# Value steps and w_down: the narrow operand as a broadcast of 32 columns

## The chip, the cores and the metric

The kernel runs on one core of one Trainium2 chip. The metric is the device time of one execution in microseconds (us). The time before is the median of 8 runs. A profile is one execution, taken by the hardware profiler; its span goes from the first to the last instruction.

## The reference

Four layers follow each other on x of shape (4, 1, 512): attention, feed-forward, attention, feed-forward. Both attention layers use the same caches and weights, and so do both feed-forward layers. Cut to what matters:

```python
def _A_ref(x, k_cache, v_cache, wq, wo):      # 32 query heads, 8 kv heads, 4096 keys, head size 128
    q = (x @ wq).reshape(B, 1, 32, 128).transpose(0, 2, 1, 3)
    k = jnp.repeat(k_cache, 4, axis=1)
    v = jnp.repeat(v_cache, 4, axis=1)
    p = softmax(einsum("bhqd,bhkd->bhqk", q, k) * 128 ** -0.5)
    o = einsum("bhqk,bhkd->bhqd", p, v)
    return o.transpose(0, 2, 1, 3).reshape(B, 1, 4096) @ wo

def _B_ref(x, w_gate, w_up, w_down):          # 512 -> 1792 -> 512
    return (gelu(x @ w_gate) * (x @ w_up)) @ w_down

x = x + _A_ref(layernorm(x), ...)
x = x + _B_ref(layernorm(x), ...)
x = x + _A_ref(layernorm(x), ...)
x = x + _B_ref(layernorm(x), ...)
```

All tensors are bf16. The batch B is 4, so each of the four sequences has its own K and V caches of 8 MB each; a K or V tile of half a kv head is 512 KB.

## The kernel before, in words

**Rounds.** The order of all work is written out by hand. Round `attend(b2, b1)` runs the first attention layer of sequence b1 and, beside it, the second attention layer of sequence b2 = b1 - 1, while the K tiles of b1 replace those of b2. K is read once for each sequence and kept in `KT` (8 kv heads x 2 tiles), V is read twice, through a ring of `KV_BUFS` = 7 buffers (two tiles of sequence 0 are kept). Before each round, `dense(b, 1)` runs the end of the output projection, the feed-forward layer and the next q for one sequence; value steps of the attention layer still open (`fill`) are put between its pieces. At the end `attend_last` runs the second attention of the last sequence, and `dense(0, 4)` the last feed-forward layer for all four sequences.

**Queues.** Nearly all loads are issued by SyncE's queue, in program order: `Keys.load` (L365) for K, `load_v` (L461) for V, `load_wq` (L122) and `load_rest` (L127 to L133) for the weights. A K load waits until the scores have read the tile it replaces, a V load until a value step has given a buffer back.

**Attention.** VectorE turns each K tile in place (L372). `scores` (L383) multiplies with moving tiles of 512 columns, four 32-column groups of the array side by side. `soft` takes the maximum (L389 to L398) and the exponential (ScalarE, L402). `soft_turn` (L410) and `soft_swap` (L429, L432) bring the probabilities to the partitions that the values need, `soft_den` (L415) and `soft_recip` (L420) give the denominators.

**Value steps.** `Values.step` takes one V tile. It is the stationary operand: 16 matmuls (L481), each with a new 128 x 128 piece of V as weights and 4 moving columns, the probabilities of the 4 query heads of that kv head at one key position per partition. Two tiles, 32 matmuls, accumulate into four columns of `ot`. VectorE multiplies with the inverse denominators and writes bf16 (L489), mostly for two kv heads at once.

**Projections.** `out_proj` (L280) and `q_rows` (L225) use the activation as weights and stream 512 columns of wo or wq, four column groups side by side; `ffn_in` does so with 448 columns of w_gate and w_up (L314), or, for four sequences at once, with the weights stationary and 4 moving columns (L307). `turn_rows` (L215) turns the rows to columns. `y_select` (L268) and `out_proj_end` (L286) finish the projection in the tile `y`.

**w_down.** `down` (L347) runs 14 x 4 matmuls with pieces of w_down stationary and `nb` moving columns, 1 in the rounds and 4 in the last layer; `add_y` (L293, L297) adds the result to x.

## Time and profile before

| what | value |
|---|---|
| median of 8 runs | 316.94 us (314.24 to 319.25) |
| the profiled execution | 319.25 us |
| its span | 317.4 us |
| TensorE matmul busy | 212.3 us (67%) |
| VectorE busy | 171.3 us (54%) |
| ScalarE busy | 28.9 us (9%) |
| moved by DMA | 114.09 MB, mean 359 GB/s over the span |
| share of DMA time used by the load queue | 94.0% |
| mean granted TensorE clock | 0.703 |

Matmul rows are read in this way: each matmul takes longer than the spacing to the next one, since they are pipelined, so the time of a row of matmuls is the spacing times their number and the length of the last one. PE is TensorE's matmuls, PEld its weight loads, DVE VectorE, ACT ScalarE, SPq the queue of SyncE that issues the loads. In the slices of the page each digit is a fortieth of the span, 7.9 us. "PEclk" is the granted clock of TensorE. The chain of waits is followed back from the last instruction; the view of waits gives, for each pair, the total time waited in us, how often, and the longest wait.

### The profile page before, as it was taken

The page shows a single profiled execution, that of the slowest core. Times are in us where ns is not written, and L with a number is a line of the kernel's source. Part 1 is how long each engine was busy: PE and PEld are TensorE (multiplying, and loading weights), DVE is VectorE, ACT ScalarE, POOL GpSimd, SP SyncE. Part 2 cuts the span into 40 slices and gives each one's busy share as a digit, 9 for nine tenths or more (in the row PEclk, how much of TensorE's full clock was granted, in tenths as well). Part 3 has the DMA queues.
Part 4 walks back from the last instruction along what each step waited for, and adds up shares of the span by engine and source line. Part 5 has one row for each costly group of instructions (what it writes and reads, how often), then busy time and mean ns, then how long its engine had stood idle before and what let it go on. Part 6 is the DMA issues. An engine that isn't in the chain of part 4 may idle for free.

```text
span 317.4 us, 8714 instructions
## 1 busy us (share of the span) xinstructions
PE 212.3 (67%) x3844; PEld 121.7 (38%) x3844; DVE 171.3 (54%) x481; ACT 28.9 (9%) x70; POOL 0.7 (0%) x6
## 2 busy tenths in 40 slices
PE   1460585243677669889864389799762877998875
PEld 0010344121324135656330246464411455645654
DVE  5575751014338896355487944454799543545133
ACT  0002001000002021200100203000202040002100
POOL 0000000000000000000000000000000000000000
PEclk9999999999998555556875555555855555559555
DMA  7999999999949999999999999999999999999900
GB/s 261 374 412 399 407 410 403 351 379 383 391 124 363 405 409 405 359 387 409 357 411 408 409 390 334 378 379 370 359 410 409 408 393 348 398 389 381 392 15 3
DMA packets 35526, 114.09 MB, mean 359 GB/s; under 512 B 3224, under 2 KB 9120, under 8 KB 35488
## 3 DMA queue, kind: packets, MB, share of 16 engines
q1 hardware_dynamic: 35488, 113.53, 94.0%
q8 instruction: 30, 0.49, 0.6%
q14 instruction: 8, 0.07, 0.1%
HBM read 113.51 MB, written 0.00 MB: 358 GB/s over the span
## 4 chain that ended last, share of the span: by engine, by line
DMA 47%; PE 24%; DVE 15%; SPq 9%; issue 3%; ACT 1%; DVEq 0%; ACTq 0%
DMA kt<-in_A_k_cache_dram 23%; DMA v<-in_A_v_cache_dram 21%; PE sc L383 6%; PE ot L481 6%; DVE kt L372 5%; PE rows L314 3%; DMA wd_sb<-in_B_w_down_dram 3%; SPq L127 3%; SPq L133 3%; PE rows L280 3%; PE y L347 2%; PE rows L225 1%; PE x L429 1%; DVE rows L215 1%; DVE pp L410 1%
## 5 line engine op out<-in xcount | busy, mean ns | idle before, releaser
L372 DVE STREAM_TRANSPOSE kt<-kt 128x1024 f32<-128x1024 f32 x64 | 75.1, 1216 | 7.4 <-DMA kt<-in_A_k_cache_dram 7.3
L481 PEld LDWEIGHTS <-v 128*128 128x128 bf16 x1920 | 59.6, 104 | 50.6 <-DMA v<-in_A_v_cache_dram 25.7
L481 PE MATMUL ot<-pe,v 128*128 128x4 bf16 x1920 | 63.7, 166 | 19.7 <-DMA v<-in_A_v_cache_dram 18.8
L383 PE MATMUL sc<-kt,qb 128*32 128x512 bf16 x512 | 63.5, 550 | 17.1 <-DVE kt L372 13.1
L215 DVE STREAM_TRANSPOSE rows<-rows 128x512 f32<-128x512 f32 (+1 forms) x23 | 16.3, 707 | 39.2 <-PE rows L225 19.7
L383 PEld LDWEIGHTS <-qb 128*32 128x32 bf16 x512 | 17.3, 116 | 47.7 <-issue 30.7
L402 ACT ACTIVATE pp<-sc,nm 128x512 bf16<-128x512 f32 x16 | 11.0, 688 | 154.5 <-DVE junk L398 154.5
L489 DVE TENSOR_TENSOR OT_bf<-ot,rden 128x8 bf16<-128x8 f32 (+1 forms) x40 | 6.5, 162 | 34.2 <-PE ot L481 33.8
L429 PE MATMUL x<-pp,ident_bf 128*32 128x128 bf16 x256 | 9.1, 284 | 23.4 <-DVE pp L410 23.2
L280 PE MATMUL rows<-wo_sb,OT_bf 128*1 128x512 bf16 (+1 forms) x136 | 17.2, 611 | 7.4 <-DMA wo_sb<-in_A_wo_dram 6.4
L225 PE MATMUL rows<-wq_sb,xn_bf 128*1 128x512 bf16 (+1 forms) x160 | 18.5, 609 | 4.9 <-DMA wq_sb<-in_A_wq_dram 4.5
L429 PEld LDWEIGHTS <-ident_bf 128*32 128x32 bf16 x256 | 6.7, 122 | 29.5 <-issue 27.8
L389 DVE TENSOR_REDUCE m<-sc 128x1 f32<-128x512 f32 x16 | 10.8, 675 | 12.3 <-PE sc L383 12.3
L410 DVE STREAM_TRANSPOSE pp<-pp 128x512 bf16<-128x512 bf16 x16 | 11.2, 701 | 4.6 <-ACT pp L402 4.3
L432 ACT CAST pe<-x 128x512 bf16<-128x512 f32 x16 | 9.4, 585 | 21.5 <-PE x L429 21.5
L347 PE MATMUL y<-H_bf,wd_sb 128*128 128x1 bf16 (+1 forms) x280 | 8.4, 165 | 2.8 <-DVE H_bf L340 1.6
L246 PE MATMUL qe<-qm,t_bf 128*128 128x64 bf16 x16 | 3.4, 212 | 10.2 <-DVE qm L236 6.2
L249 DVE TENSOR_TENSOR qb<-qe,amask 128x256 bf16<-128x256 f32 x16 | 6.8, 424 | 5.4 <-PE qe L246 5.4
L347 PEld LDWEIGHTS <-wd_sb 128*128 128x128 bf16 x280 | 8.0, 103 | 4.1 <-DMA wd_sb<-in_B_w_down_dram 3.0
L225 PEld LDWEIGHTS <-xn_bf 128*1 128x1 bf16 (+1 forms) x160 | 4.3, 108 | 13.2 <-issue 12.1
L415 PE MATMUL den<-zx,mean_f 128*128 128x16 f32 x32 | 8.9, 357 | 0.0
L420 DVE RECIPROCAL rden<-den 128x16 f32<-128x16 f32 x16 | 4.0, 251 | 8.8 <-PE den L415 8.3
(78 smaller groups left out, 124.4 us busy)
## 6 DMA issues: line engine op xcount, KB each, us to landing
v<-in_A_v_cache_dram SPq DMA_DIRECT2D x118, 512.0 KB, 8.7
kt<-in_A_k_cache_dram SPq DMA_DIRECT2D x64, 512.0 KB, 11.0
wq_sb<-in_A_wq_dram SPq DMA_DIRECT2D x2, 2048.0 KB, 7.8
wo_sb<-in_A_wo_dram SPq DMA_DIRECT2D x4, 1024.0 KB, 12.0
kt<-in_A_v_cache_dram SPq DMA_DIRECT2D x8, 512.0 KB, 9.2
wg_sb<-in_B_w_gate_dram SPq DMA_DIRECT2D x1, 1792.0 KB, 13.5
wu_sb<-in_B_w_up_dram SPq DMA_DIRECT2D x1, 1792.0 KB
wd_sb<-in_B_w_down_dram SPq DMA_DIRECT2D x1, 896.0 KB, 16.1
```

The costliest lines, as they stand in the source:

```text
L127: dq.dma_start(out=wo_sb[:, i * n:(i + 1) * n], in_=wo_dram[:, i * n:(i + 1) * n])
L215: nc.vector.transpose(out=rows[:, :n], in_=rows[:, :n])
L225: nc.tensor.matmul(rows[j * QS:j * QS + nb, :], lhsT=xn_bf[:, k, bs], rhs=w, start=(k == 0), stop=(k == KD - 1))
L280: nc.tensor.matmul(rows[r0:r0 + lhsT.shape[-1], :], lhsT=lhsT, rhs=wo_sb[:, i, :], start=(start and n < QD), stop=(stop and n >= hp - QD))
L347: nc.tensor.matmul(y[:, k], lhsT=wd_sb[:, c, k * P:(k + 1) * P], rhs=H_bf[:, c, :], start=(c == 0 and k == 0), stop=(c == KF - 1), skip_gr ...
L372: nc.vector.transpose(out=words, in_=words)
L383: nc.tensor.matmul(sc[s * QS:(s + 1) * QS], lhsT=qb[:, w0:w0 + 2 * W], rhs=kt[:, :, be // 2, :, be % 2], start=(t == 0 and be == 0), stop= ...
L389: nc.vector.tensor_reduce(out=m[:], in_=sc.rearrange("p c j -> p (c j)"), axis=AX.X, op=ALU.max)
L402: nc.scalar.activation(out=pp[:], in_=sc[:], func=ACT.Exp, bias=nm[:, 0:1], scale=scale, accum_out=ls[:])
L410: nc.vector.transpose(out=flat, in_=flat)
L429: nc.tensor.matmul(x[a * QS:(a + 1) * QS, s], lhsT=ident_bf[:, s * QS:(s + 1) * QS], rhs=pT[:, a], start=True, stop=True, skip_group_check ...
L481: nc.tensor.matmul(self.ot[:, s % 2], lhsT=v[:, i, :], rhs=pe[:, s, c, :], start=(c == 0), stop=(c == C - 1), skip_group_check=True)
```

## The change

Both kinds of matmul with a narrow moving operand get 32 moving columns. In a value step the 4 columns are read eight times over by a broadcast dimension of stride 0, and in `down` the 1 or 4 columns 32 or 8 times. The PSUM tiles grow by the same factor, from 8 to 64 fp32 per partition for `ot`, from 4 or 16 to 128 for `y` of `down`, and hold as many equal copies of the result; one copy is read. The number of instructions, the stationary operands, the order and the loads are as before.

```diff
+    WIDE = 8
...
     def down(nb, H_bf):
-        y = ps_sm.tile([P, KD, nb], FP32, name="y", tag="sm")
+        n = WIDE * rep // nb
+        y = ps_sm.tile([P, KD, n, nb], FP32, name="y", tag="sm")
         for c in range(KF):
             for k in range(KD):
-                nc.tensor.matmul(y[:, k], lhsT=wd_sb[:, c, k * P:(k + 1) * P], rhs=H_bf[:, c, :],
+                nc.tensor.matmul(y[:, k], lhsT=wd_sb[:, c, k * P:(k + 1) * P],
+                                 rhs=H_bf[:, c, :].unsqueeze(1).broadcast_to([P, n, nb]),
                                  start=(c == 0 and k == 0), stop=(c == KF - 1), skip_group_check=True)
-        return y
+        return y[:, :, 0]
...
-                    self.ot = ps_ot.tile([P, 2, rep], FP32, name="ot", tag="ot")
+                    self.ot = ps_ot.tile([P, 2, WIDE, rep], FP32, name="ot", tag="ot")
...
-                    nc.tensor.matmul(self.ot[:, s % 2], lhsT=v[:, i, :], rhs=pe[:, s, c, :],
+                    rhs = pe[:, s, c, :].unsqueeze(1).broadcast_to([P, WIDE, rep])
+                    nc.tensor.matmul(self.ot[:, s % 2], lhsT=v[:, i, :], rhs=rhs,
                                      start=(c == 0), stop=(c == C - 1), skip_group_check=True)
...
-                        in0=self.ot[:, s0 % 2:s0 % 2 + m], in1=rden[:, s0:s0 + m], op=ALU.mult)
+                        in0=self.ot[:, s0 % 2:s0 % 2 + m, 0], in1=rden[:, s0:s0 + m], op=ALU.mult)
```

## The prediction

> **What bounds the kernel now.** I read the page first: its slices, its costliest groups, and the waits of the DMA queue.

> ```profile
> PEclk9999999999998555556875555555855555559555
> DMA  7999999999949999999999999999999999999900
> GB/s 261 374 412 399 407 410 403 351 379 383 391 124 363 405 409 405 359 387 409 357 411 408 409 390 334 378 379 370 359 410 409 408 393 348 398 389 381 392 15 3
> ...
> L481 PEld LDWEIGHTS <-v 128*128 128x128 bf16 x1920 | 59.6, 104 | 50.6 <-DMA v<-in_A_v_cache_dram 25.7
> L481 PE MATMUL ot<-pe,v 128*128 128x4 bf16 x1920 | 63.7, 166 | 19.7 <-DMA v<-in_A_v_cache_dram 18.8
> ```

> ```profile
> SPq L461 <- PE ot L481: 72.2, 60, 3.1
> ```

> Transfers bound it: 113.5 MB run at about 408 GB/s wherever nothing holds them, 278 us of a 317.4 us span. TensorE has two roles beside that. It frees the V buffers (the second fence: the queue waits for ot), so its pauses let the rate fall to 330 to 390 GB/s, and it carries the end, where the last 16 us move no data.

> The clock row needs care. Before 101 us no throttling is on record and the row shows 9, yet the score matmuls of 0 to 88 us have a median of 628 ns, the same as at clock 0.50, against 398 ns at 153 to 157 us under clock 1.00. So TensorE is at half speed for nearly the whole kernel. What raises the clock? I cut the trace into stretches of 3.41 us at the places where the clock changes:

> ```profile
> 190.20:193.62 3.42, 3.27 (x57) 1.94 (x50) 2.23 (x8) 1.76 (x6) 0.00 (x0) 0.50 0.95 290
> 217.51:220.92 3.41, 3.41 (x40) 1.12 (x32) 0.74 (x2) 0.00 (x0) 0.00 (x0) 0.50 1.00 375
> 220.92:224.33 3.41, 3.28 (x70) 1.57 (x59) 1.83 (x7) 0.85 (x3) 0.00 (x0) 1.00 1.01 329
> ...
> 296.01:299.42 3.41, 3.41 (x96) 2.31 (x88) 0.18 (x1) 0.00 (x0) 0.00 (x0) 0.50 1.03 413
> 299.42:302.84 3.42, 3.42 (x90) 2.27 (x87) 0.18 (x1) 0.00 (x0) 0.00 (x0) 0.50 0.62 246
> ```

> The first column after the comma is busy PE, the third from the right its clock. Two stretches are busy to the last ns, 217.51 and 296.01. After the first the clock is 1.00, after the second it stays at 0.50. The first holds scores and q rows, 512 columns wide. The second holds value steps of 4 columns and some rows.

> [...] The row says that it is columns streamed that count. At 1.2 columns per ns, taken from groups of four parallel score matmuls that pass 512 columns in about 427 ns, 217.51 streams 100% of its time; 296.01 streams some 80 value matmuls x 3.3 ns + 12 x 107 ns (512 columns, four at a time) = 1.55 us, 45%. The highest cold stretch that released nothing streams some 65% (190.20), the lowest that did about 66 to 89% (149.2 and 139.0). I go by the row: threshold about two thirds.

> **Part 1: the wider operand.** Each of 2048 value matmuls streams 32 columns for 4; 224 of w_down 32 for 1, and 56 in the last layer 32 for 4. Instruction counts, waits and DMAs stay the same.

> ```profile
> 299.71 1.87 PE L481 MATMUL ot<-pe,kt 128*128 128x4 bf16 x64
> 311.89 1.63 PE L347 MATMUL y<-H_bf,wd_sb 128*128 128x4 bf16 x56 [0.42 <-DVE H_bf L340]
> 274.68 1.66 PE L347 MATMUL y<-H_bf,wd_sb 128*128 128x1 bf16 x56
> 99.74 1.75 PE L481 MATMUL ot<-pe,v 128*128 128x4 bf16 x64
> 281.69 1.90 PE L383 MATMUL sc<-kt,qb 128*32 128x512 bf16 x16
> 222.11 2.07 PE L383 MATMUL sc<-kt,qb 128*32 128x512 bf16 x32
> ```

> Spacing cold: (1.87 - 0.166) / 63 = 27.0 ns; for w_down at 4 columns (1.63 - 0.166) / 55 = 26.6, at one column (1.66 - 0.165) / 55 = 27.2. Three columns fewer are not cheaper, so it is the weight load (or the issue) that sets 27 ns and the stream lies under it. Clock 1.00 (99.74): (1.75 - 0.166) / 63 = 25.1. Thirty-two columns take 32 / 1.2 = 26.7 ns cold, 13.3 warm.

> No row has 128 weight columns with a stream that long, so both bounds. Low: all hidden, 27 ns, cost 0. High: load and stream one after the other, 26.7 + 26.7 = 53 ns. [...] The nearest row is 281.69: four groups, each matmul with a new weight load of 116 ns on record, at (1.90 - 0.61) / 3 = 0.43 us per group, the stream alone; its weights are only 32 columns wide. Two rows (one against four columns, and the score groups) show overlap, so I take 27 ns and keep 53 for a rival.

> The last matmul of a chain does end later: 28 more columns, 23 ns cold or 12 warm. The waits view has 22 waits of the evacuation (L489) and 5 of XX (L293, L297) for it: 27 x about 18 = **+0.5 us**.

> The broadcast reads each 8-byte run eight times. x<-pp (L429) also reads runs of four elements: 16 matmuls in 0.62 us are (0.62 - 0.284) / 3 = 0.11 us per 128 columns, full rate (107 ns). A repeated address stands in no row; cost 0, at most the rival below. The evacuations L489 and L293 read with a stride: 8 outputs take 161 ns and 4 take 165, so layout and size hardly count: 0, bounds -0.1 to +0.3 us over 49 instructions. The larger PSUM tiles (256 and 512 bytes per partition) need no further wait.

> **Part 2: what the streaming does to the clock.** With 16 x 26.7 = 427 ns per value step: 296.01 goes to 80 x 26.7 + 1280 = 3.4 us (100%); 183.38 and 186.79 (48 value matmuls each and 12 scores) to 1280 + 1280 = 2.56 us (75%, from 42); 121.9 from 58 to 91%. All cross two thirds, so the clock should come up about 35 us earlier in the middle rounds and for the tail. It should then stay up longer: warm stretches of 39% streaming kept it (156.1), 11% lost it (98.0), and the dense part would lie at 25 to 40%.

> What warm is worth, per piece: 16 scores 1.90 against (2.07 - 0.38) / 8 x 3 + 0.38 = 1.0 us, so 0.9 less, and as much for 16 of L280 and L225 (1.88); 16 of L314 0.75 less; x and den 0.2 each. Value steps gain 2 ns per matmul, next to nothing. On the stretch 189.5 to 222 us of one round, PE on the chain could shed L280 1.5, L314 1.5, L225 0.9, scores 0.9 and 0.6 of small ones, 5.4 us.

> Only what the transfers lost can be won back. Lost time is 8 x (1 - rate / 408) for each 8 us:

> ```profile
> 184.00:192.00 8.00, 7.07 (x144) 4.16 (x144) 3.72 (x11) 1.08 (x3) 0.00 (x0) 0.50 1.00 361
> 192.00:200.00 8.00, 6.97 (x158) 4.91 (x148) 2.35 (x9) 2.16 (x5) 0.00 (x0) 0.50 0.98 352
> ```

> These give 0.9 + 1.1; 128 to 160 us gives 2.4, 184 to 224 4.2, 256 to 296 2.5: 9.1 us. The hole at 88 to 96 us (5.5) stays: no stretch ahead of it crosses the threshold. A pause of the value steps such as 189.95 to 193.01 would shrink by L280 0.87 + x and den 0.4 of 3.06, about 40%: 0.4 x 9.1 = **-3.6 us**. The tail: three groups of 8 of L280 (1.02 each, 0.45 less), x, den, st and the last four rows 0.2 each, 2.2 us if warm from 295, and one stretch late **-1.5**. Bounds of part 2: 0 (no clock, or the end only waits for bytes) to -9.1 - 2.2 = -11.

> Sum: 0 + 0.5 - 3.6 - 1.5 = -4.6 us. The profiled execution took 319.25 with a span of 317.4, the longest of the eight; 314.6 for it. From the median of 316.94: **312.3 us**.

> **Rivals.** A, hidden streams and a warm clock as above, 0.52: 312.3, own range 308 to 315.5. B, hidden but without effect on the end, 0.18: transfers bound the rounds and the gate follows something else; for it, 94% of queue time is taken; against it, the tail moves no data. 316.94 + 0.5 - 1 = 316.5. C, weight load and stream take turns, 0.22: place L481 and L347, price +26.7 ns each when cold. The chain of waits lists 592 value and 236 w_down matmuls; from 289 us on 312 of them, 8.3 us, have no transfer to hide behind; of the other 516 (13.8 us) I count half, since the piece after them often is a transfer at full rate. Less half of A's gain: 316.94 + 8.3 + 6.9 - 2.5 = 329.6. It decides against the change from about 10 ns per matmul on: 312 x 10 + 516 x 5 = 5.7 us, more than A brings. D, a few ns of handover (27 to about 33), 0.08: 316.94 + 312 x 6 ns + 516 x 3 ns + 0.5 - 2.5 = 318.4.

> **Numbers.** A measurement of this kernel tells about 1% from no change, 313.8 to 320.1. A gives faster 0.40, same 0.12; B 0.02, 0.15, slower 0.01; C slower 0.22; D 0.01, 0.03, 0.04. Together 0.43, 0.30, 0.27. The range of 8 in 10 leaves out A's best tenth and the upper half of C: 307 to 330.

> **What would show it.** Right: ot matmuls of 128x32 with 27 ns spacing; clock 1.00 after about 190 and after 299 us; L280 and L314 means well under 600 ns; rates over 390 at 184 to 224 us; value steps hardly faster. C: 64 value matmuls at about 3.5 us. B: clock up but the same GB/s and end. It fails if streams don't hide, if the gate doesn't count them, or if earlier buffers only meet a queue that is already full.

## The result and the profile after

The changed kernel takes 311.69 us (median of 22 runs, 308.59 to 315.72) against 316.59 (59 runs of the kernel before): ratio 0.983, 95% interval 0.981 to 0.986, or 4.9 us. Times are medians of all runs, while the ratios leave out the slow ones, those over 1.5% above the fastest run of their kernel. The prediction said 312.3. The profiled execution of the changed kernel took 311.11 us with a span of 309.3. The profile of before happened to be 2.7 us above the median of its kernel, so the two spans differ by 8.1 us, and some 3 us of that are the spread of one execution.

The page of the changed kernel: granted clock, transfers, and the widened groups. Line numbers have moved by 1 to 4: L481 is L485, L347 is L349, L383 is L386.

```profile
PEclk9999997555559558758775567789755795679685
DMA  7999999999949999999999999999999999999910
GB/s 247 399 412 405 407 411 406 354 370 395 380 165 334 405 405 408 407 407 407 402 401 409 411 405 400 375 397 396 403 407 409 409 407 406 390 389 363 405 40 3
...
L485 PE MATMUL ot<-pe,v 128*128 128x32 bf16 x1920 | 64.8, 182 | 22.2 <-DMA v<-in_A_v_cache_dram 20.2
...
L485 PEld LDWEIGHTS <-v 128*128 128x128 bf16 x1920 | 57.9, 100 | 50.0 <-DMA v<-in_A_v_cache_dram 29.8
```

The clock row is now mixed from 43 us on. The value matmuls stream eight times the columns and are 16 ns longer each, 182 for 166, with no more busy time to speak of (64.8 for 63.7 us); TensorE as a whole is busy for 201.1 us where it was 212.3. The rates of the middle and late slices, which fell to 334 to 359, stay at 375 or more from the 14th to the 36th slice. The queue still waits for value steps as long as before (72.2 us before), so the V buffers are still what it lacks most:

```profile
SPq L464 <- PE ot L485: 71.7, 69, 2.8
```

Stretches of 3.41 us, cut at the changes of the clock (first number after the comma busy PE, third from the right the clock, last the GB/s):

```profile
199.84:203.26 3.42, 3.42 (x56) 1.35 (x52) 2.71 (x14) 0.21 (x1) 0.00 (x0) 0.50 1.00 399
203.26:206.67 3.41, 3.27 (x108) 2.91 (x101) 1.07 (x6) 0.00 (x0) 0.00 (x0) 1.00 1.03 406
...
288.59:292.00 3.41, 3.41 (x93) 2.48 (x97) 0.43 (x2) 0.30 (x1) 0.00 (x0) 0.50 1.03 413
292.00:295.41 3.41, 3.29 (x96) 2.28 (x96) 0.26 (x2) 0.00 (x0) 0.00 (x0) 1.00 0.70 280
```

288.59 does nearly the same work as 296.01 did before (93 matmuls for 96) and is as busy, 3.41 of 3.41 us. There the clock stayed at 0.50, here it comes up: busy time alone doesn't decide. TensorE's matmuls in order of time show what that is worth and what it isn't:

```profile
288.73 1.02 PE L281 MATMUL rows<-wo_sb,OT_bf 128*4 128x512 bf16 x8
...
290.13 1.87 PE L485 MATMUL ot<-pe,kt 128*128 128x32 bf16 x64
291.93 0.62 PE L281 MATMUL rows<-wo_sb,OT_bf 128*4 128x512 bf16 x8
292.48 1.78 PE L485 MATMUL ot<-pe,kt 128*128 128x32 bf16 x64
```

```profile
204.63 1.91 PE L349 MATMUL y<-H_bf,wd_sb 128*128 128x32 bf16 x56
```

The groups of 8 of L281 go from 1.02 to 0.62 us, the 64 value matmuls only from 1.87 to 1.78. w_down takes 1.91 us there, at full clock, where it took 1.66 before at half clock and 1.55 at full (the round at 143 us). At half clock it is no slower: in the first dense part its first 28 matmuls take 1.03 us from 80.46 us on, (1.03 - 0.19) / 27 = 31 ns each, as (1.91 - 0.19) / 55 = 31 at full. The transfers in the two stretches of 8 us that the prediction showed at 361 and 352 GB/s:

```profile
184.00:192.00 8.00, 5.86 (x132) 4.12 (x132) 3.79 (x15) 3.25 (x8) 0.00 (x0) 0.79 1.02 405
192.00:200.00 8.00, 5.60 (x138) 4.21 (x142) 2.22 (x13) 0.00 (x0) 0.00 (x0) 0.78 1.01 373
```

### The profile page after: what moved, and what is told of

It reads as the page before. It is cut to its first block, busy times and chain, and to the rows that moved or that the text cites. A ratio compares the mean times of both kernels' runs of the same rounds, so it can differ in the third digit from the quotient of the medians.

```text
span 309.3 us, 8714 instructions
## 1 busy us (share of the span) xinstructions
PE 201.1 (65%) x3844; PEld 118.4 (38%) x3844; DVE 170.1 (55%) x481; ACT 29.0 (9%) x70; POOL 0.7 (0%) x6
## 4 chain that ended last, share of the span: by engine, by line
DMA 39%; PE 27%; DVE 21%; SPq 8%; issue 4%; ACT 1%; DVEq 0%; ACTq 0%
DMA v<-in_A_v_cache_dram 21%; DMA kt<-in_A_k_cache_dram 14%; DVE kt L375 8%; PE ot L485 6%; PE sc L386 6%; DMA wd_sb<-in_B_w_down_dram 3%; SPq L128 3%; PE rows L315 3%; SPq L134 3%; PE y L349 3%; PE rows L281 2%; DVE rows L216 2%; PE rows L226 2%; DVE qb L250 2%; DVE pp L413 1%
## 5 line engine op out<-in xcount | busy, mean ns | idle before, releaser
L485 PE MATMUL ot<-pe,v 128*128 128x32 bf16 x1920 | 64.8, 182 | 22.2 <-DMA v<-in_A_v_cache_dram 20.2
L485 PEld LDWEIGHTS <-v 128*128 128x128 bf16 x1920 | 57.9, 100 | 50.0 <-DMA v<-in_A_v_cache_dram 29.8
L386 PE MATMUL sc<-kt,qb 128*32 128x512 bf16 x512 | 59.2, 513 | 15.3 <-DVE kt L375 11.2
L386 PEld LDWEIGHTS <-qb 128*32 128x32 bf16 x512 | 17.0, 111 | 43.9 <-issue 29.5
L432 PE MATMUL x<-pp,ident_bf 128*32 128x128 bf16 x256 | 7.8, 251 | 23.2 <-DVE pp L413 23.2
L226 PE MATMUL rows<-wq_sb,xn_bf 128*1 128x512 bf16 (+1 forms) x160 | 15.7, 529 | 4.8 <-DMA wq_sb<-in_A_wq_dram 4.4
L281 PE MATMUL rows<-wo_sb,OT_bf 128*1 128x512 bf16 (+1 forms) x136 | 13.9, 501 | 7.3 <-DMA wo_sb<-in_A_wo_dram 6.3
L432 PEld LDWEIGHTS <-ident_bf 128*32 128x32 bf16 x256 | 5.8, 108 | 28.9 <-issue 26.7
L349 PE MATMUL y<-H_bf,wd_sb 128*128 128x32 bf16 x280 | 9.7, 192 | 2.6 <-DVE H_bf L341 1.6
L349 PEld LDWEIGHTS <-wd_sb 128*128 128x128 bf16 x280 | 9.0, 102 | 4.0 <-DMA wd_sb<-in_B_w_down_dram 2.9
L294 DVE SCALAR_TENSOR_TENSOR XX<-XX,y 128x4 f32<-128x4 f32 x8 | 1.3, 158 | 12.9 <-PE y L349 8.9
L315 PE MATMUL rows<-wu_sb,xn_bf 128*1 128x448 bf16 x64 | 6.5, 555 | 2.9 <-DMA wu_sb<-in_B_w_up_dram 2.9
```

Source lines behind the costliest of these rows:

```text
L226: nc.tensor.matmul(rows[j * QS:j * QS + nb, :], lhsT=xn_bf[:, k, bs], rhs=w, start=(k == 0), stop=(k == KD - 1))
L281: nc.tensor.matmul(rows[r0:r0 + lhsT.shape[-1], :], lhsT=lhsT, rhs=wo_sb[:, i, :], start=(start and n < QD), stop=(stop and n >= hp - QD))
L315: nc.tensor.matmul(rows[j * QS:j * QS + nb, :KF * QS], lhsT=xn_bf[:, k, bs], rhs=w[:, j], start=(k == 0), stop=(k == KD - 1))
L349: nc.tensor.matmul(y[:, k], lhsT=wd_sb[:, c, k * P:(k + 1) * P], rhs=H_bf[:, c, :].unsqueeze(1).broadcast_to([P, n, nb]), start=(c == 0 an ...
L386: nc.tensor.matmul(sc[s * QS:(s + 1) * QS], lhsT=qb[:, w0:w0 + 2 * W], rhs=kt[:, :, be // 2, :, be % 2], start=(t == 0 and be == 0), stop= ...
L432: nc.tensor.matmul(x[a * QS:(a + 1) * QS, s], lhsT=ident_bf[:, s * QS:(s + 1) * QS], rhs=pT[:, a], start=True, stop=True, skip_group_check ...
```

## The experiments

Two theories. **Clock**: what the value steps stream raises TensorE's clock, the wide matmuls (scores, projections, q rows) get shorter, buffers come back earlier, and the transfers lose less. **Width**: something else about the wider operand or its tile brings the time, and the clock goes along with it. Each ratio is to the kernel before on the same chip, with its 95% interval; the experiments ran on three chips, on which the kernel before took 315.78 to 316.94 us, so compare ratios rather than times. "Time at full clock" is taken from 100 us on, where the granted clock is on record in every profile. "Lost" is what the transfers lose against 408 GB/s by the prediction's formula, in the three stretches 128 to 160, 184 to 224 and 256 to 288 us of the profile.

**Two columns for eight: 16.** `WIDE = 4` in the value steps, w_down as in the change.

> The value steps stream 16 columns (w_down 32 as in the change). Theory (columns streamed in a stretch of 3.4 us decide, threshold about two thirds): half the streaming, 80 value matmuls of 13.3 ns and 1.28 us of rows are 69% at the end, 48 of them and 1.28 us of scores 56%; the clock comes up less often, spacing stays 27 ns cold and 25 warm: 313 to 316 us, mean clock between the two kernels. Rival (any widening brings the gain, not its amount): 311.7.

Measured: 318.29 us, ratio 1.003 (1.000 to 1.006). None of the gain is left, more than was expected: full clock for 24 us, as before (29), where the change has 83. The spacing is 27 ns as at 32 columns, the broadcast and the layout are of the same kind, and w_down is as wide. What differs is the amount streamed, and with it the size of `ot`. The stretch 184 to 200 us and its projection in this kernel:

```profile
184.00:192.00 8.00, 6.98 (x145) 4.05 (x142) 3.67 (x14) 1.09 (x3) 0.00 (x0) 0.50 1.03 407
192.00:200.00 8.00, 6.86 (x152) 4.89 (x151) 2.52 (x9) 2.16 (x5) 0.00 (x0) 0.50 1.02 367
```

```profile
189.77 1.88 PE L281 MATMUL rows<-wo_sb,OT_bf 128*1 128x512 bf16 x16
```

Half clock throughout, and 16 matmuls of L281 in 1.88 us as before. The transfers lose 9.5 us as before (8.8), where the change loses 3.3. This speaks for the clock and against the width as such.

**More than eight: 40, 48 and 64 columns.** `WIDE = 10`, `12`, `16`, w_down as in the change.

> The value steps stream 40 columns, w_down 32 as in the change. Theory: 33 ns per matmul cold, 25 warm; clock between the 0.724 of 32 columns and the 0.797 of 48; 310.5 to 311.7 us. It tells whether the time still falls with the clock between 32 and 48 columns or lies on a flat floor: same within 0.3% as the changed kernel if flat.

> The value steps stream 48 columns. Theory (spacing is the larger of weight load and stream): 48 / 1.2 = 40 ns cold, 25 ns warm (20 under the issue spacing of 25); cold stretches pay 13 ns per matmul, but the clock is held more firmly since a warm step streams 80% of its time: 311 to 314 us. If load and stream took turns: 67 ns cold and 33 warm, over 318.

> The value steps stream 64 columns. Theory: spacing 53 ns cold, 27 warm; mean clock over 0.8; the tail starts its value steps at half clock and pays up to 80 x 26 ns: 312 to 317 us. If load and stream took turns: 80 ns cold, 40 warm, over 322. This also tells from where on the width costs more than the clock brings.

| columns | spacing at 0.50, ns | at 1.00, ns | us at full clock after 100 us | L281 mean, ns | lost, us | time, us | ratio (95%) |
|---|---|---|---|---|---|---|---|
| 4 (before) | 27 | 25 | 29 | 611 | 8.8 | 316.59 | 1 |
| 16 | 27 | 25 | 24 | 582 | 9.5 | 318.29 | 1.003 (1.000 to 1.006) |
| 32 (change) | 27 | 25 | 83 | 501 | 3.3 | 311.69 | 0.983 (0.981 to 0.986) |
| 40 | 33 | 25 | 102 | 472 | 4.6 | 309.67 | 0.979 (0.974 to 0.983) |
| 48 | 40 | 25 | 127 | 425 | 2.1 | 310.62 | 0.985 (0.979 to 0.991) |
| 64 | 53 | 31 | 143 | 419 | 3.2 | 312.96 | 0.989 (0.986 to 0.992) |

(Spacings are medians of the starts in each profile; L281 was L280 before.) A value step of 16 matmuls at half clock, with 48 and with 64 columns:

```profile
198.06 0.82 PE L485 MATMUL ot<-pe,v 128*128 128x48 bf16 x16
```

```profile
199.70 1.02 PE L485 MATMUL ot<-pe,v 128*128 128x64 bf16 x16
```

(0.82 - 0.21) / 15 = 41 ns and (1.02 - 0.22) / 15 = 53 ns: the stream alone, 48 / 1.2 and 64 / 1.2, with the prediction's 1.2 columns per ns. The 80 ns at 64 columns that were expected if load and stream took turns aren't there. The time at full clock rises with the width from 16 columns on, from 24 to 143 us. The time of the kernel is lowest at 32 to 48 columns; 40 and 48 came out just under what was expected of them. Whether 40 beat the change is not settled: on one chip the medians of six runs each are 309.67 and 312.20 us, but the runs overlap (308.06 to 311.87 and 309.45 to 313.52), as do the intervals (0.981 to 0.991 for the change, below). At 64 the gain is smaller, though the time at full clock is the longest and the transfers lose no more than with the change (3.2 for 3.3 us); that steps at half clock then cost 53 ns for 27 is the likely reason, not one shown apart.

**One part alone: the value steps.** `down` as in the kernel before.

> One part alone: the value steps stream 32 columns, w_down keeps its 1 or 4. Theory (the gain is the clock, raised by the columns that the value steps stream): 2048 of 2328 widened matmuls are still there, so the clock stays up as in the changed kernel, and w_down comes every 27 ns again and not every 31, 0.26 us less in each of four dense parts: 310.5 to 311.5 us, 56 w_down matmuls in about 1.6 us. Rival (w_down's own streams are needed to hold the clock through the dense part): 313 to 314.5, and fewer stretches at clock 1.00 between 140 and 160, 204 and 220, 268 and 285 us.

Measured: 313.25 us, 0.991 (0.987 to 0.995): slower than the change by 0.7% of the time before, 2.3 us, though w_down itself is faster (against the second measurement of the change, 0.986 below, it is 0.5%, and the intervals overlap). The rival's figures hold. The transfers lose 5.8 us where the change loses 3.3. The q rows that follow w_down in that profile, and the transfers around them:

```profile
208.59 2.45 PE L226 MATMUL rows<-wq_sb,xn_bf 128*1 128x512 bf16 x16
```

```profile
208.00:216.00 8.00, 7.52 (x132) 3.45 (x133) 4.68 (x20) 0.00 (x0) 0.00 (x0) 0.82 0.93 308
```

In the changed kernel the q rows take 1.07 us at 207.80, and that stretch has 398 GB/s. After w_down the clock fell back within one stretch of 3.4 us in all three rounds here (142.7, 207.5, 272.4); in two profiles of the change (the second is of the run repeated below) it held for two stretches or more in five of six. In the sixth, of the second profile, the clock fell back at 207.8 us as it does here, the q rows at 208.29 took 1.88 us, and the rate fell:

```profile
208.00:216.00 8.00, 7.32 (x148) 3.78 (x148) 5.07 (x22) 0.00 (x0) 0.00 (x0) 0.80 0.99 344
```

Both are executions of the changed kernel, and only the edges of the clock lie elsewhere: clock 1.00 and 398 GB/s in one, 0.80 and 344 in the other. So in these profiles the clock mostly outlasts the dense part with the wide w_down, whose 56 matmuls take 1.91 us between value steps that are wide too, and doesn't with the narrow one.

**The other part alone: w_down.** `down` as in the change, value steps with 4 columns.

> The other part alone: w_down streams 32 columns, the value steps keep 4. Theory: 1.5 us of streaming in a dense part with thin value steps around it stays under two thirds of 3.4 us, the clock stays as in the kernel before, and w_down pays 4 to 5 ns per matmul: 317 to 318 us. Rival (w_down brings the gain, as it stands right ahead of the q rows and the scores): 312 to 314 us.

Measured: 320.07 us, 1.009 (1.006 to 1.012), full clock for 21 us. Alone w_down's streams raise nothing and only cost, as the theory said, but more than it said: its rows are together 1.0 us longer than before, which is 0.3%. The rest, some 0.6%, isn't explained; in the profile the kernel before has a stretch at full clock at 142.4 that is missing here.

**w_down's broadcast in runs of four.** VectorE writes H four times in the rounds:

```diff
-        H_bf = small.tile([P, KF, nb], BF16, name="H_bf", tag="H_bf")
-        nc.vector.tensor_tensor(out=H_bf[:], in0=hu, in1=sq[:], op=ALU.mult)
+        H_bf = small.tile([P, KF, rep // nb, nb], BF16, name="H_bf", tag="H_bf")
+        wide = [P, KF, rep // nb, nb]
+        nc.vector.tensor_tensor(out=H_bf[:], in0=hu.unsqueeze(2).broadcast_to(wide),
+                                in1=sq[:].unsqueeze(2).broadcast_to(wide), op=ALU.mult)
```

> The changed kernel, but VectorE writes each column of H four times (in the rounds), so that w_down's broadcast repeats runs of four elements, 8 bytes, as the value steps do, and not one 2-byte element 32 times. Theory (a repeated single element is read at about 1 ns each whatever the clock): spacing 25 to 27 ns for 31, 56 matmuls in about 1.6 us for 1.92, 310.5 to 311.5 us. Rival (the 31 ns come from elsewhere, such as 32 columns written into a tile of 512 bytes per partition): still 31 ns and the time of the changed kernel, 311.7.

```profile
206.38 1.57 PE L351 MATMUL y<-H_bf,wd_sb 128*128 128x32 bf16 x56
```

The spacing is 25 ns, (1.57 - 0.18) / 55, at full clock and 27 at half, for 31 at either in the change: the 31 ns came with the single 2-byte element repeated 32 times, and went with it. The changed kernel shows it itself: in its last layer, where w_down repeats runs of four into a tile of the same size, the same 56 matmuls take 1.66 us at half clock, for 1.63 before.

```profile
303.82 1.66 PE L349 MATMUL y<-H_bf,wd_sb 128*128 128x32 bf16 x56 [0.42 <-DVE H_bf L341]
```

The time is 311.83 us, 0.987 (0.982 to 0.991), the same as the change within the intervals; the 1.0 us by which w_down is shorter in three dense parts (in the first it waits for its weights) did not come out.

**The first dense part filled.** In addition 10 matmuls of 512 columns of a constant, never read, stand where the other dense parts have value steps:

```diff
-        fill = (lambda n: None) if prev is None else prev.step
+        fill = pads if prev is None else prev.step
...
+    def pads(n):
+        for _ in range(n):
+            nc.tensor.matmul(pad[:], lhsT=t32_bf.rearrange("p a i -> p (a i)"),
+                             rhs=t32_bf.rearrange("p a i -> p (a i)").unsqueeze(1).broadcast_to([P, 4, P]),
+                             start=True, stop=True, skip_group_check=True)
```

> As the run with H written four times, and with 10 extra matmuls of 512 columns of a constant tile, never read, in the first dense part (sequence 0), where the other dense parts have value steps between their pieces and this one has none. Theory: the stretches ahead of 88 us then stream over two thirds, the scores and q rows at 88 to 94 us run at clock 1.00 (1.0 us for 16 and not 1.9), K loads start 1 to 2.5 us earlier, and the hole in the transfers at 88 to 96 us shrinks by as much: 308.5 to 310. Rival (the hole is VectorE's chain, or the extra matmuls delay what stands behind them): no gain or up to 1 us slower, 310.5 to 312.

Measured: 311.82 us, 0.987 (0.981 to 0.993), no gain. The clock did what was expected. TensorE, the queue's issues and the transfers there:

```profile
89.07 1.08 PE L389 MATMUL sc<-kt,qb 128*32 128x512 bf16 x16 [0.30 <-DVE qb L250]
```

```profile
93.63 1.47 SPq L371 DMA_DIRECT2D kt<-in_A_k_cache_dram  x1
```

```profile
88.00:96.00 8.00, 5.86 (x98) 2.63 (x99) 4.21 (x14) 1.09 (x3) 0.00 (x0) 1.00 0.54 161
```

The scores take 1.08 for 1.90 us, but two K loads behind them took 1.23 and 1.47 us to issue where the median is 0.33, and the eighth K load starts at 96.3 us, as without the fill (96.2). The hole gives 161 GB/s, for 141 in the changed kernel and 118 in the run with H written four times. Neither the chain of VectorE nor a delay of the work behind, the rival's two reasons, is needed to explain the late eighth load: the queue's own issuing took 2.0 us more for those two. Why they took so long stays open.

**The clock by other means.** Narrow value steps, and after each a matmul of 384 columns, except in the last round. It adds work that the reference doesn't have.

```diff
+                if b < B - 1 or not last:
+                    nc.tensor.matmul(self.pad, lhsT=v[:, CH - 1, :], rhs=v[:, :3, :],
+                                     start=False, stop=True, skip_group_check=True)
```

> The kernel before, all operands narrow, with one extra matmul of 384 columns after each value step except those of the last round: it streams the 384 newest V values into columns of the ot tile that are never read. Theory (the gain is the clock, whoever streams): clock and rates in the rounds rise as with the change, L280 and L314 there fall under 500 ns, at a price of up to 0.35 us per step that isn't hidden; the tail stays cold: 312 to 316 us. Rival (the width of the value matmuls itself brings the gain): clock up, no gain in rates, 318 us or more.

```profile
192.00:200.00 8.00, 7.86 (x145) 4.98 (x137) 3.16 (x10) 2.22 (x6) 0.00 (x0) 0.50 0.99 371
```

```profile
L486 PE MATMUL ot<-v 128*128 128x384 bf16 x112 | 50.2, 448 | 0.0
```

Measured: 324.79 us, 1.030 (1.022 to 1.037); both expectations missed. The clock hardly rose (42 us at full clock, L280 mean 582 ns), so the run doesn't tell the theories apart. The extra matmuls (L486) raise TensorE's busy time from 212.3 to 234.0 us, which is the likely cost. Nor did they stream enough: a 3.4 us stretch holds fewer of the longer steps, and those from 182.9 to 193.1 us, busy all the time, stream 72 to 74% of it, in the band where the clock comes up in one stretch and not in the next (see below).

**The last round narrow.** 4 columns in `attend_last`, beside the changed kernel once more.

> The changed kernel once more, as the common yardstick for the three runs beside it, and as a second profile, so that what the two profiles have in common can be told from what one execution does: about 311.7 us, ratio 0.980 to 0.987, clock 1.00 over 10 to 13 stretches. If the place of the stretches is fixed by the kernel, their edges stay within 1 us of the first profile; if the gate's 3.4 us grid runs free, they shift by up to 3.4 us.

> The changed kernel with 4 columns again in the 256 value matmuls of the last round. Theory with the split of the prediction (3.6 us in the rounds, 1.5 in the tail): the clock falls back to 0.50 from about 285 us on as in the kernel before, the three groups of 8 of L281 take 0.95 us each again, 1 to 1.5 us slower than the changed kernel, 312.7 to 313.5. Rival (all of the gain comes from the transfers in the rounds, and the end only waits for bytes): 311.7, the same as the changed kernel.

Measured: the changed kernel 312.20 us, 0.986 (0.981 to 0.991); with the narrow last round 311.00, 0.983 (0.979 to 0.988). The second profile of the change has 85 us at full clock after 83; its edges lie 1.1 us later or 2.3 earlier, one shift of the grid of 3.41 us: it lay at different places of the kernel in the two executions. The start of the last round's values in the kernel before, the change and the narrow last round:

```profile
291.69 1.79 PE L481 MATMUL ot<-pe,v 128*128 128x4 bf16 x64 [0.36 <-ACT pe L432]
```

```profile
284.85 1.85 PE L485 MATMUL ot<-pe,v 128*128 128x32 bf16 x64 [0.36 <-ACT pe L435]
```

```profile
282.90 1.80 PE L486 MATMUL ot<-pe,v 128*128 128x4 bf16 x64 [0.36 <-ACT pe L435]
...
292.71 1.02 PE L281 MATMUL rows<-wo_sb,OT_bf 128*4 128x512 bf16 x8
```

From there to the end of the span, in that order: 317.4 - 291.7 = 25.7, 309.3 - 284.9 = 24.4, 308.6 - 282.9 = 25.7 us. The tail is 1.3 us shorter with the change and loses that when narrow. In the times this doesn't show: with intervals of about 0.5% either way, 1.3 us (0.4%) could be there or not. What the tail is worth in the median stays open.

**Both widened to 48.** The run with H written four times, with `WIDE = 12` for value steps and w_down alike.

> 48 columns in both the value steps and w_down, with H written four times so that w_down repeats runs of four. Theory: w_down comes every 25 ns warm and streams 20 of them, so it holds the clock and costs no more than in the kernel before; value steps as in the run of 48 columns: clock near 0.8, 309 to 311 us, 0.3 to 0.8% under the changed kernel. Rival (more clock brings nothing once the transfers run at 400 GB/s): 311.5 to 312, the same as the changed kernel.

Measured: 313.77 us, 0.989 (0.983 to 0.995): not faster than the change, against what was expected. What w_down's spacing was in this run is not shown; an estimate from the value steps of 48 columns is 40 ns at half clock, for 31 in the change. No version is clearly better than the change; 40 columns come nearest.

## Why the prediction was right

**Hidden streams: right.** 27 ns cold (clock 0.50) and 25 warm (1.00) for the value steps, as taken. The high bound of 53 ns fell. At 40, 48 and 64 columns the cold spacing, 33, 40 and 53 ns, is the stream alone, and from 4 to 32 columns it stays at 27. Warm it stays at 25 ns from 4 to 48 columns and is 31 at 64. Whether the weight load or the issue sets the 27 and 25 ns, which the prediction left open, no run shows.

**The clock follows columns streamed: right in these runs, the two thirds a little low.** The kernel at 16 columns, with 24 us at full clock for 83, speaks for the amount. The prediction took two thirds of 3.41 us. It called two of its stretches busy to the last ns; its last line, 299.42, was so too and also stayed at 0.50, which makes its case stronger. Worked out for every stretch of three profiles (before and two of the change; four column groups side by side count once), those at half clock that raised it stream about 70% of their time or more (149.2 us of before 66% by the prediction's count), those that didn't at most 74%. Counted so, the 69% expected at 16 columns fell just short, and the whole gain was gone. The count isn't exact: in the other profiles one stretch raised the clock at 63% (16 columns, 120.7 us), and others at 75% did not (w_down alone, 214.9 us).

**Warm pieces: right.** 8 of L281 0.40 us shorter (0.45 predicted), 16 scores 0.8, value steps 2 ns per matmul. The longer last matmul is 16 ns, for 18 taken.

**The transfers: right cause, too small a size.** With the prediction's own formula, 128 to 160 us lose 0.4 for 2.4 us, 184 to 224 lose 1.4 for 4.2 and 256 to 288 1.5 for 2.2: 5.5 us won where 3.6 was the term. The second profile of the change gives 5.8. The execution of before was a long one, so this is the upper side. One sign came only in part: of the five stretches at 184 to 224 us one stayed under 390 GB/s, at 373. The hole at 88 to 96 us stayed, as said.

**The tail: in the rows, not in the times.** 1.3 us in the profile for 1.5 predicted; the narrow last round does not confirm it.

**The step that was missed** is the broadcast: "A repeated address stands in no row; cost 0". Value steps with runs of four cost 0 per matmul, 27 and 25 ns as before. But w_down in the rounds takes 31 ns per matmul, 0.25 us more than before at half clock and 0.36 at full in each of three dense parts, and 0.09 in the first, where it waits for its weights (2.98 for 2.89 us): about 1 us. The wide w_down is still worth having for the clock, as the run without it is 0.5 to 0.7% slower. The sum came out near with some luck, because the transfers gave 2 us more than forecast and w_down took 1.

Rival B (no effect on the end) fell with the times; rivals C and D with the spacing. The link from the clock to the time rests on the series of widths: between 4 and 16 columns neither the time at full clock rises (29 and 24 us) nor the time falls (ratio 1.003), at 32 both do (83 us, 0.983). The step from shorter matmuls to fuller transfers is read from profiles: those with 29 us or less at full clock after 100 us (before, 16 columns, w_down alone) lose 8.8 to 9.5 us in the three stretches, those with 75 us or more 2.1 to 5.8 (the run with extra matmuls, 42 us, loses 10.2). The two executions of the changed kernel at 208 to 216 us come nearest to the clock changed alone; the run meant to raise it without widening the steps didn't raise it enough.

## What to carry to other kernels

Ask how many columns TensorE streams, and not only how long it is busy: at 296.01 us in the kernel before it was busy for 3.41 of 3.41 us with thin matmuls and stayed at clock 0.50, and with wide ones at 288.59 in the change it was as busy and went to 1.00. Look at whether the spacing of thin matmuls depends on their width at all. Here it was 27 ns at half clock from 4 to 32 columns, so that value steps read in runs of four elements could be repeated eight times for 16 ns at the end of a chain; w_down, with one element over and over, took 31 ns, and 25 to 27 in runs of four. The gain appeared in other instructions, here the wide scores (16 in 1.08 us for 1.90) and projections (8 of L281 in 0.62 for 1.02). Look for what a faster engine releases (the ring of V buffers), and measure the width, since half of it brought nothing (ratio 1.003 at 16 columns).
